# Zeroing the rows behind an expert buffer's overflow in another stage, as copies from DRAM to DRAM

## The chip, the core and the metric

The kernel runs on one core of a Trainium2 chip. The metric is device time in microseconds (us) of one execution. The core has five instruction queues that run side by side and meet only through semaphores: PE (matrix multiply, with its weight loads shown as PEld), DVE (vector), ACT (activation), POOL (general, and here the indirect DMAs) and SP, which only issues DMAs. The DMAs of all queues are carried by the same 16 DMA engines.

## The reference, cut to what matters

```python
x = attention(q, k_pooled, v_pooled)             # 4608 tokens x 512
logits = x @ w_gate + log1p(exp(x @ w_noise)) * noise
top2 = two best of 8 experts per token, softmax over the two -> gates
for e in range(8):                               # mixture of experts
    out[mask_e] += gate * (relu(x[mask_e] @ w1[e]) @ w2[e])   # 512 -> 1024 -> 512
h = out @ w_in                                   # 512 -> 2048, float64 weights
return (h * cos(h)) @ w_out                      # 2048 -> 512
```

## The kernel before

There are three stages.

**Attention, about 0 to 340 us.** Four groups of nine token tiles. The code works in 20 units `u` of one or two tiles; the order of the work inside a unit is a fixed list, and small steps for the next group are filled in between. SP loads k, v and q of later groups; POOL scatters each finished token row to its two experts' places in the DRAM buffer `xs` (indirect DMAs, line 588). Between units, SP also writes zeros. `zero_x` (line 218) clears the ends of the eight expert areas in `xs`. `zero_y(i)` (line 222) is called twice after each of the units 4 to 12, 18 times in all. Each call writes 384 rows of 2 KB, 768 KB, into the part of `yb` that begins at row `YS`; the source is the zero tile `zt` in on-chip memory (SBUF), 128 partitions each giving three rows. The 18 calls cover all 54 x 128 overflow rows.

**Experts, about 340 to 1075 us.** Each expert has 1216 places (`CAP`), worked as jobs of 512, 512 and 192 rows. Tokens beyond an expert's places are overflow: a loop (line 811) runs once for every 128 of them, `nov` times in all (a count that is read at run time), and writes its result to `yb` from row `YS` on. In a job, `mm1` (line 611, eight blocks `f`) makes `ph`, ACT turns it into the high half of `ht` (line 887) and DVE into the low half (line 888); `mm2` (line 900) makes `py`, which ACT scales (903) and stores into `yb` (905). The jobs' inputs come by `DMA_TRANSPOSE xt<-xs` (867), the experts' weights by lines 129 to 133.

The list `work` holds the calls of `mm1` and `mm2` in order, two blocks of the next job's `mm1` between two tiles of `mm2`. `begin` is the PE time at which each of them should start by a count of columns, and `at(t, f)` puts step `f` behind the first piece of work that begins at or after `t`. That way the background steps are spread: the splitting of the next expert's weights, and `bg`, the preparation of the last stage's float64 weights. A chunk of these is loaded by SP into `yg` (956), POOL makes `tm` from it (966), DVE converts it (973 to 976), ACT and DVE split it into `ty` (1022, 1023), and SP stores that into `wind` or `woutd` (1024). All queues run in order, so a background step that waits holds up whatever stands behind it on its engine.

**Last stage, about 1075 us to the end.** Per four tiles POOL gathers the two expert rows of each token from `yb` (1097; the first two groups from the rows of the 512-row jobs, the later ones from all of `yb`), then the two dense layers follow on PE (1315 and 1352).

SP's and ACT's DMAs take eight completion semaphores in turn. A DMA is issued only when the one that had its semaphore before it has landed.

Of the kernel before, what the change touches and what calls it, by code (L numbers as in the profile page):

```python
# [8 lines left out]
F32 = mybir.dt.float32  # L9
# [11 lines left out]
NTOK, DM, E, F, DFF = 4608, 512, 8, 1024, 2048  # L21
# [3 lines left out]
YS = E * CAP  # L25
ZROW = 960
OVT = 54
# [8 lines left out]
def tile_attn_moe_ffn(ctx: ExitStack, tc: tile.TileContext, q, k, v, wgate, wnoise, noise,  # L36
                      w1, w2, win, wout, out):
    nc = tc.nc
    V, A, PL, PE, SP = nc.vector, nc.scalar, nc.gpsimd, nc.tensor, nc.sync

    def dap(src, offset, dims):
        return bass.AP(tensor=src.tensor, offset=src.offset + offset, ap=dims)

    const = ctx.enter_context(tc.tile_pool(name="const", bufs=1))
    dram = ctx.enter_context(tc.tile_pool(name="dram", bufs=1, space=DR))
    ctx.enter_context(tc.manual_schedule())

    xs = dram.tile([E * ER, 2 * DM], F16, name="xs")
    yb = dram.tile([YS + 128 * OVT, DM], F32, name="yb")
    idx = const.tile([128, G, 2, R], I32, name="idx")  # L50
    yidx = const.tile([128, G, 2, R], I32, name="yidx")
    gates = const.tile([128, G, 2, R], F32, name="gates")
# [20 lines left out]
    def load_kv(g, which):  # L73
        src, dst = ((k, KT), (v, VT))[which]
        t = ow.tile([128, 5, 2, 512], F32, name="w1", bufs=2)
        for c in range(5):
            n = 128 if c < 4 else 64
            for h in range(2 if which and c == 4 else 1):
                SP.dma_start(t[64 * h:64 * h + n, c, :, :],
                             dap(src, 2 * g * S * 512 + 65536 * c, [[512, n], [S * 512, 2], [1, 512]]))  # L80
        dst[g] = t
# [84 lines left out]
    def w2_room(e):  # L166
        return SW[:, 0:4096].bitcast(F16) if e % 2 == 0 else WP[1]
# [46 lines left out]
    zt = ac.tile([128, 2048], F16, name="zt")  # L214
    V.memset(zt, 0.0)

    def zero_x():
        SP.dma_start(dap(xs, ZROW * 1024, [[2048, 128], [ER * 1024, 8], [1, 2048]]),
                     zt[:, None, :].to_broadcast([128, 8, 2048]))

    def zero_y(i):
        SP.dma_start(dap(yb, (YS + 384 * i) * 512, [[512, 128], [65536, 3], [1, 512]]),
                     zt.bitcast(F32)[:, None, 0:512].to_broadcast([128, 3, 512]))

    def pow2(pool, m, bits, nm):

# [356 lines left out]
    def scatter(g, r):  # L583
        def f():
            xr = XR.pop(g * R + r)
            for kk in range(2):
                PL.memset(spacer, 0.0)
                st = PL.indirect_dma_start(
                    out=xs[:, :], out_offset=bass.IndirectOffsetOnAxis(ap=idx[:, g, kk, r:r + 1], axis=0),
                    in_=xr.rearrange("p s a h d -> p (s a h d)"), in_offset=None)  # L590
                for o in SCAT:
                    tc.declare_no_dep(st.ins, o.ins, reason="each slot is written once")
                if "load" in EARLY:
                    tc.declare_no_dep(st.ins, EARLY["load"].ins, reason="rows of later pairs lie behind the first chunk")
                SCAT.append(st)
        return f
# [33 lines left out]
    def with_ups(gt, fs):  # L630

        return gt[:6] + [early_up(f) for f in fs] + gt[6:9] + [early_lo(f) for f in fs] + gt[9:]
# [30 lines left out]
    def mix(a, b):  # L663

        n = len(a) + len(b)
        out, i, j = [], 0, 0
        while i < len(a) or j < len(b):
            if j >= len(b) or (i < len(a) and i * len(b) <= j * len(a)):
                out.append(a[i])
                i += 1  # L670
            else:
                out.append(b[j])
                j += 1
        return out
# [14 lines left out]
    def go():  # L689
        k_ = -(-len(fill) // left[0])  # L690
        left[0] = max(left[0] - 1, 1)
        for f in fill[:k_]:
            f()
        del fill[:k_]

    for u in range(NU):
        g, r, n = UNITS[u]
        it = u % 5
        if it == 0:
            a = []  # L700
            if g + 1 < G:
                pk, kt_, pv, sv = setup_steps(g + 1)
                a = pk + pv[:2]
                for i in range(4):
                    a += kt_[i:i + 1] + pv[i + 2:i + 3]
                a += sv
                if g + 2 < G:
                    a.append(lambda g=g: (load_kv(g + 2, 0), load_kv(g + 2, 1)))
            if g == G - 1:
                a = p2  # L710
            fill += mix(a, late)
            late = []
        if g == G - 2 and it == 2:
            p1, p2 = prep_steps(0, "w1"), prep_steps(0, "w2")
            p1.pop(0)()
            p2.pop(0)()
        if g == G - 2 and it == 3:
            fill = mix(fill, p1)
        if g == G - 1 and it in CUTS:
            r0, r1 = CUTS[it]  # L720
            gt = gating(g, r0, r1)
            gt.pop(0)()
            fill += with_ups(gt, (0, 1) if it == 3 else (2, 3)) + [scatter(g, r_) for r_ in range(r0, r1)]
        left[0] = ORDER.count("G") * ((5 if g < G - 1 or it > 2 else 3) - it)
        if g == G - 1 and it == 3:
            left[0] = 6
        for op in ORDER:
            k_ = int(op[1:] or 0)
            if op == "A0":

                while first_v:
                    first_v.pop(0)()
            if op[0] == "G":
                go()
            elif op[0] == "S":
                scores(u + 2, k_)
            elif op[0] == "E":
                expo(u + 2, k_)
            elif op[0] == "N":
                soft_sum(u + 1)  # L740
            elif op[0] == "T":
                e_tr(u, k_)
            elif op[0] == "A":
                av(u, k_ // 2, k_ % 2)
            else:
                q_tr(u + 3, k_)
        if u == 2:
            zero_x()
        if 4 <= u <= 12:
            zero_y(2 * u - 8)  # L750
            zero_y(2 * u - 7)
        if it == 4:
            assert not fill
            if g + 2 < G:
                load_q(g + 2)
            if g == G - 2:
                early_load()
            if g < G - 1:
                late = gating(g, 0, R)
                late.pop(0)()  # L760
                late += [scatter(g, r_) for r_ in range(R)]
# [48 lines left out]
    nov = nc.values_load(novi[0:1, 0:1], min_val=0, max_val=OVT)  # L810
    with tc.For_i(0, nov, 1) as i:
# [4 lines left out]
        p = PT[0]()  # L816
# [10 lines left out]
        z = wp.tile([128, 1024], F16, name="x2h", bufs=2)  # L827
# [265 lines left out]
    def gather(c, i):  # L1093
        g, r = CHF[c][i]
        yg = wp.tile([128, 2, 512], F32, name="yg", bufs=4)
        for kk in range(2):
            PL.indirect_dma_start(out=yg[:, kk, :], out_offset=None, in_=yb[0:512 * E * (c + 1), :] if c < 2 else yb[:, :],
                                  in_offset=bass.IndirectOffsetOnAxis(ap=yidx[:, g, kk, r:r + 1], axis=0))
        CB["yg", c, i] = yg

# [120 lines left out]
    for j in range(1, NJ + 1):  # L1221
        up_ = [(mm1, j, f) for f in range(8)] if j < NJ else []
        dn = []
        if j > 0:
            e, c = JOBS[j - 1]
# [10 lines left out]
    first = {e: min(i for i, w_ in enumerate(work) if w_[0] is mm1 and JOBS[w_[1]][0] == e) for e in range(E)}  # L1236
    first[E] = len(work)
    sched = [[] for _ in work]
    begin = [0.0]
# [3 lines left out]
    def at(t, f):  # L1243

        sched[min(i for i in range(len(work)) if begin[i] >= t)].append(f)
# [11 lines left out]
    for f in bg:  # L1257
        for r0, r1 in rest:
            if r0 <= b0 < r1:
                b0 += r1 - r0  # L1260
        at(b0, f)
        b0 += each
    FW = {}

    def load_out(i):
        def f():
            t = w2_room(i).rearrange("p (k n) -> p k n", n=512)
            FW.setdefault("out", []).append(t)
            SP.dma_start(t.rearrange("p k f -> p (k f)"), woutd[:, i, :])
        return f  # L1270

    def load_in(i):
        def f():
            o, n = ((0, 10), (10, 9), (19, 9))[i]
            t = ow.tile([128, n, 1024], F16, name="st" if i else "w1", bufs=2)
            FW.setdefault("in", []).extend(t[:, j, :] for j in range(n))
            SP.dma_start(t, wind.rearrange("p o s k f -> p (o s k) f")[:, o:o + n, :])
# [10 lines left out]
    o = work.index((mm2, JOBS.index((E - 1, 0)), 3))  # L1288
# [18 lines left out]
    def prod(c, q_, n, ps, start):  # L1307
        a_, b_ = PRODS[n]
        x = xt_tile(c, b_).rearrange("p (i s k) n -> p i s k n", i=2, s=2)
        for h in range(2):  # L1310
            f = 128 * (2 * q_ + h)
            o = ps[:, 256 * h:256 * h + 256].rearrange("p (i n) -> p i n", i=2)
            for k_ in range(2):
                for j, (sa, sb) in enumerate(((0, 0), (0, 1), (1, 0))):
                    PE.matmul(o, FW["in"][4 * a_ + 2 * sa + k_][:, f:f + 128], x[:, :, sb, k_, :],  # L1315
                              start=(start and h == 0 and k_ == 0 and j == 0), stop=(k_ == 1 and j == 2), skip_group_check=True)
# [27 lines left out]
    def down(c, q_, b, tt, h):  # L1344

        def f():
# [4 lines left out]
            for i, (a_, b_) in enumerate(((0, 0), (0, 1), (1, 0))):  # L1351
                PE.matmul(ps, g[:, 2 * b + a_, 256 * h + 128 * tt:256 * h + 128 * tt + 128], FW["out"][b_][:, k_, :],  # L1352
                          start=(q_ == 0 and b < 2 and h == 0 and i == 0), stop=(q_ == 3 and b > 1 and h == 1 and i == 2))
# [105 lines left out]
```

## Time and profile before

| | us |
|---|---|
| median of 3 runs | 1832.84 |
| lowest and highest | 1831.86, 1833.45 |
| the profiled execution | 1835.67 |
| its span (first to last instruction) | 1833.9 |
| PE busy in the span | 1737.3 (95%) |
| DVE, ACT, POOL busy | 1063.2, 927.0, 424.3 |

The profiled execution lies 2.8 us above the median. PE's chain of work makes up most of the span: of the chain that ended last, 76% is PE. DMA engines are busiest in the first tenth of the span and then between 20 and 100% over the experts stage. DMA-issuing instructions are not counted as busy time of an engine; the trace shows when each was issued, and how long the issuing queue was held by it.

### The profile page before, as it was taken

Reading aid. Unit: us, or ns where it says so; the run is one execution under the profiler, and the core shown is the slowest. Engines: PE = TensorE matmul, PEld = TensorE weight load, DVE = VectorE, ACT = ScalarE, POOL = GpSimd, SP = SyncE. Lnnn points to the kernel's source line nnn. Section 1 sums busy time; section 2 is a strip of 40 time slices with the busy share of each in tenths; the row PEclk is TensorE's granted clock in tenths of the full one; section 3 lists DMA queues with packets and bytes.
Section 4 is the critical chain, followed back from the end, with each engine's and each line's share of the span. In section 5 each row is a group of like instructions: output and inputs, shape, how many; then the busy total and the mean of one; then the engine's idle time right before and its main releaser. Section 6 shows DMA issues by size and latency. Waiting matters only on the chain.

```text
span 1833.9 us, 28207 instructions
## 1 busy us (share of the span) xinstructions
PE 1737.3 (95%) x11113; PEld 1024.7 (56%) x11113; DVE 1063.2 (58%) x2018; ACT 927.0 (51%) x1843; POOL 424.3 (23%) x458
## 2 busy tenths in 40 slices
PE   5977777899999999999999998999999999999999
PEld 3655554355444644464445545666666666666665
DVE  7685765363567376525775134756656556565633
ACT  4765553232324233323333235777776777777765
POOL 1225437100001000000110012424333342433222
PEclk9888778899999999999999999999999999999999
DMA  9977424548353837466463635304232141322200
GB/s 277 307 261 273 174 92 161 153 159 229 107 180 117 243 107 219 125 178 167 132 212 90 215 127 144 79 32 87 63 71 59 52 87 41 75 64 64 41 24 24
DMA packets 233208, 243.49 MB, mean 133 GB/s; under 512 B 154352, under 2 KB 167664, under 8 KB 232432
## 3 DMA queue, kind: packets, MB, share of 16 engines
q1 hardware_dynamic: 210544, 183.97, 35.7%
q0 software_dynamic: 11520, 37.76, 6.3%
q10 hardware_dynamic: 11008, 19.93, 3.1%
q8 instruction: 88, 1.44, 0.3%
q14 instruction: 48, 0.39, 0.1%
HBM read 127.06 MB, written 78.12 MB: 112 GB/s over the span
## 4 chain that ended last, share of the span: by engine, by line
PE 76%; DVE 3%; ACT 1%; issue 1%; ACTq 0%; DVEq 0%
PE ph L1352 20%; PE py L900 19%; PE ph L611 18%; PE py L1315 15%; PE pt L1315 3%; PE py L915 1%; DVE w L159 1%; DVE ht L888 0%; DVE x L1112 0%; ACT w L158 0%; DVE amw L139 0%; DVE ty L1327 0%; DVE ty L974 0%; DVE ty L976 0%; DVE ty L975 0%
## 5 line engine op out<-in xcount | busy, mean ns | idle before, releaser
L611 PE MATMUL ph<-xt,w 128*128 128x512 f16 (+1 forms) x2208 | 387.1, 333 | 1.0 <-DVE ht L888 1.0
L1352 PE MATMUL ph<-sw,ht 128*128 128x512 f16 x1152 | 383.0, 379 | 0.0
L611 PEld LDWEIGHTS <-w 128*128 128x128 f16 x2304 | 214.4, 98 | 187.3 <-issue 6.1
L1342 POOL TENSOR_TENSOR ht<-ty,ht 128x512 f16<-128x512 f32 x144 | 183.6, 1281 | 479.9 <-ACT ht L1341 324.0
L900 PEld LDWEIGHTS <-ht 128*128 128x128 f16 x1632 | 159.4, 98 | 187.6 <-DVE ht L888 0.7
L888 DVE SCALAR_TENSOR_TENSOR ht<-ph,ht 128x512 f16<-128x512 f32 (+2 forms) x184 | 104.0, 568 | 259.5 <-ACT ht L887 259.4
L1352 PEld LDWEIGHTS <-ht 128*128 128x128 f16 x1728 | 169.3, 98 | 152.1 <-issue 0.8
L1352 PE MATMUL ph<-w,ht 128*128 128x512 f16 x576 | 218.6, 379 | 0.0
L1315 PEld LDWEIGHTS <-st 128*128 128x128 f16 x1872 | 183.2, 98 | 54.4 <-issue 3.5
L900 PE MATMUL py<-w,ht 128*128 128x512 f16 x864 | 191.9, 379 | 0.0
L887 ACT ACTIVATE ht<-ph 128x512 f16<-128x512 f32 (+2 forms) x184 | 91.5, 498 | 164.2 <-PE ph L611 148.5
L900 PE MATMUL py<-sw,ht 128*128 128x512 f16 x768 | 171.2, 379 | 0.2 <-DVE ht L888 0.2
L903 ACT ACTIVATE yt<-py,ysc 128x512 f32<-128x512 f32 x72 | 49.3, 685 | 229.6 <-PE py L900 229.5
L1315 PE MATMUL py<-xt,st 128*128 128x256 f16 x1040 | 139.3, 273 | 3.1 <-ACT ht L1405 3.1
L1327 DVE SCALAR_TENSOR_TENSOR ty<-ty,k,ht 128x512 f32<-128x512 f32 x108 | 93.7, 868 | 81.7 <-ACT ty L1321 80.0
L1336 DVE SCALAR_TENSOR_TENSOR ty<-ty,ht 128x512 f32<-128x512 f32 x108 | 74.7, 692 | 108.7 <-ACT ty L1333 105.6
L1315 PEld LDWEIGHTS <-w 128*128 128x128 f16 x1152 | 113.1, 98 | 39.6 <-issue 3.8
L1332 ACT ACTIVATE ty<-ty,k 128x512 f32<-128x512 f32 x144 | 102.8, 714 | 21.4 <-DVE ty L1327 21.3
L1315 PE MATMUL py<-w,st 128*128 128x256 f16 x832 | 111.8, 273 | 0.0
L1321 ACT ACTIVATE ty<-ht,k 128x512 f32<-128x512 f32 x108 | 77.4, 717 | 67.3 <-DVE ht L1406 33.8
L1341 ACT ACTIVATE ht<-ty 128x512 f16<-128x512 f32 x144 | 89.5, 622 | 34.9 <-DVE ty L1336 34.3
L966 POOL TENSOR_TENSOR tm<-yg 128x512 f32<-128x512 f32 x32 | 33.7, 1053 | 297.0 <-DVE x L976 183.5
(262 smaller groups left out, 2366.8 us busy)
## 6 DMA issues: line engine op xcount, KB each, us to landing
yb<-yt ACTq DMA_DIRECT2D x72, 256.0 KB
yg<-in_moe_w_in_dram SPq DMA_DIRECT2D x32, 512.0 KB
yg<-in_moe_w_out_dram SPq DMA_DIRECT2D x32, 512.0 KB
st<-in_moe_w_dram SPq DMA_DIRECT2D x7, 2048.0 KB
yb<-zt SPq DMA_DIRECT2D x18, 768.0 KB
st<-in_moe_w_dram SPq DMA_DIRECT2D x8, 1536.0 KB
w<-in_k_dram SPq DMA_DIRECT2D x16, 512.0 KB
w<-in_v_dram SPq DMA_DIRECT2D x16, 512.0 KB
```

Source lines behind the costliest of these rows:

```text
L611: PE.matmul(ps[:, 0:n], w[:, a_, k_, 128 * f:128 * f + 128], xt[:, 4 * b_ + k_, 0:n], start=(i == 0), stop=(i == 11))
L887: A.activation(t[:, 0], p, AF.Relu)
L888: V.scalar_tensor_tensor(t[:, 1], p, 0.0, t[:, 0], op0=OP.max, op1=OP.subtract)
L900: PE.matmul(ps[0:m], ht[:, a_, f, 128 * t:128 * t + m], w[:, b_, f, :], start=(i == 0), stop=(i == 23))
L1315: PE.matmul(o, FW["in"][4 * a_ + 2 * sa + k_][:, f:f + 128], x[:, :, sb, k_, :], start=(start and h == 0 and k_ == 0 and j == 0), stop=(k_ ...
L1321: A.activation(y, h, AF.Identity, bias=CB["k4", c][:, 0:1])
L1327: V.scalar_tensor_tensor(y, y, CB["k4", c][:, 0:1], h, op0=OP.subtract, op1=OP.subtract)
L1332: A.activation(y, y, AF.Sin, scale=CB["k4", c][:, 1:2])
L1336: V.scalar_tensor_tensor(UB[b][3], UB[b][3], CC, UB[b][2], op0=OP.subtract, op1=OP.mult)
L1341: A.activation(g[:, 2 * b, :], y, AF.Copy)
L1342: PL.tensor_sub(g[:, 2 * b + 1, :], y, g[:, 2 * b, :])
L1352: PE.matmul(ps, g[:, 2 * b + a_, 256 * h + 128 * tt:256 * h + 128 * tt + 128], FW["out"][b_][:, k_, :], start=(q_ == 0 and b < 2 and h == ...
```

## The change

`zero_y` now writes to a place that is known only at run time: the 384 rows that begin `nov * 128` rows behind `YS + 384 * i`. So the rows that the overflow loop wrote are left alone and as many rows behind the old end of the buffer are written; `yb` is made 54 x 128 rows longer for that. The source is a new 256 KB DRAM buffer `zd` of zeros, filled once from `zt` after unit 2, and each of the 18 copies reads it three times. The copies are placed with `at` in the experts stage, evenly between the begin of expert 1 and the begin of expert 7. The gathers of the last stage read the old extent of `yb`.

```diff
-    yb = dram.tile([YS + 128 * OVT, DM], F32, name="yb")
+    yb = dram.tile([YS + 256 * OVT, DM], F32, name="yb")
+    zd = dram.tile([128, DM], F32, name="zd")
...
+    def zero_d():
+        SP.dma_start(zd[:, :], zt.bitcast(F32)[:, 0:512])
+
+    ZY = []
+
     def zero_y(i):
-        SP.dma_start(dap(yb, (YS + 384 * i) * 512, [[512, 128], [65536, 3], [1, 512]]),
-                     zt.bitcast(F32)[:, None, 0:512].to_broadcast([128, 3, 512]))
+        def f():
+            z = SP.dma_start(yb[bass.ds(nov * 128 + (YS + 384 * i), 384), :].rearrange("(k p) d -> k p d", p=128),
+                             zd[None, :, :].to_broadcast([3, 128, DM]))
+            for o in ZY:
+                tc.declare_no_dep(z.ins, o.ins, reason="rows behind those of the overflow")
+            ZY.append(z)
+        return f
...
         if u == 2:
             zero_x()
-        if 4 <= u <= 12:
-            zero_y(2 * u - 8)
-            zero_y(2 * u - 7)
+            zero_d()
...
-in_=yb[0:512 * E * (c + 1), :] if c < 2 else yb[:, :],
+in_=yb[0:512 * E * (c + 1), :] if c < 2 else yb[0:YS + 128 * OVT, :],
...
         b0 += each
+    z0, z1 = begin[first[1]], begin[first[E - 1]]
+    for i in range(18):
+        at(z0 + (z1 - z0) * i / 18, zero_y(i))
     FW = {}
```

No instruction of PE, DVE, ACT or POOL changes its place; SP's queue is the one that differs. In the attention stage of the kernel before, the zero writes stand between the loads of q (`st<-in_q_dram`), k and v:

```order
L79 DMA w_1007<-in_v_dram 64x2x512 x2
L222 DMA yb<-zt 128x3x512 x2
L88 DMA st<-in_q_dram 64x8x576 x2
L222 DMA yb<-zt 128x3x512 x8
L79 DMA w_1971<-in_k_dram 128x2x512 x4
L79 DMA w_1971<-in_k_dram 64x2x512
```

In the changed kernel the same place of SP's queue holds the loads alone (the numbers in the names are buffer numbers):

```order
L80 DMA w_1009<-in_v_dram 64x2x512 x2
L89 DMA st<-in_q_dram 64x8x576 x2
L80 DMA w_1963<-in_k_dram 128x2x512 x4
L80 DMA w_1963<-in_k_dram 64x2x512
```

The ten writes of this place are gone from it, and the loads follow one another.

In the experts stage, where expert 7's weights are loaded and the chunks of `w_out` are prepared, SP's queue before is:

```order
L131 DMA st<-in_moe_w_dram 128x3x1024
L133 DMA st<-in_moe_w_dram 64x1024 x2
L1024 DMA woutd<-ty 256x1x512
L956 DMA yg<-in_moe_w_out_dram 128x1024
L129 DMA st<-in_moe_w_dram 128x8x512
L1024 DMA woutd<-ty 256x1x512
L956 DMA yg<-in_moe_w_out_dram 128x1024
```

The same place in the changed kernel:

```order
L132 DMA st<-in_moe_w_dram 128x3x1024
L134 DMA st<-in_moe_w_dram 64x1024 x2
L1033 DMA woutd<-ty 256x1x512
L965 DMA yg<-in_moe_w_out_dram 128x1024
L130 DMA st<-in_moe_w_dram 128x8x512
L1033 DMA woutd<-ty 256x1x512
L229 ISA
L229 DMA yb<-zd 3x4x16384
L965 DMA yg<-in_moe_w_out_dram 128x1024
```

A register instruction and a copy (the sixteenth of the 18) now stand directly ahead of a `yg` load. The copy's shape is three outer rows of four pieces of 16384 numbers of four bytes, where the write before had 128 outer rows. The next copy stands in the same way ahead of a `yg` load, and the last one ahead of an `xt` load:

```order
L965 DMA yg<-in_moe_w_out_dram 128x1024
L1033 DMA woutd<-ty 256x1x512
L229 ISA
L229 DMA yb<-zd 3x4x16384
L965 DMA yg<-in_moe_w_out_dram 128x1024
L1033 DMA woutd<-ty 256x1x512
L965 DMA yg<-in_moe_w_out_dram 128x1024
L1033 DMA woutd<-ty 256x1x512 x3
L229 ISA
L229 DMA yb<-zd 3x4x16384
L876 DMA_TRANSPOSE xt<-xs 128x8x512
```

## Rows read from the trace of the kernel before

**Rows 1.** Busy time by stage: PE, PEld, DVE, ACT, POOL, PEclk, DMA share, GB/s.

```profile
0.00:350.00 350.00, 265.25 (x2235) 175.52 (x2236) 232.52 (x684) 184.68 (x653) 133.85 (x208) 0.83 0.66 210
350.00:1075.00 725.00, 723.86 (x3928) 364.37 (x3926) 395.25 (x661) 225.99 (x360) 39.97 (x41) 1.00 0.56 166
1075.00:1834.00 759.00, 748.15 (x4954) 484.81 (x4951) 435.44 (x673) 516.38 (x831) 250.52 (x210) 1.00 0.26 65
```

**Rows 2.** PE's waits, 340 to 1075 us: us in total, times, longest.

```profile
PE py L900 <- DVEq L811: 3.8, 1, 3.8
PE ph L611 <- DVE ht L888: 1.0, 1, 1.0
PE py L900 <- DVE ht L888: 0.2, 1, 0.2
```

**Rows 3.** The one wait for a DMA in the attention stage, in PE's timeline.

```profile
30.48 1.06 PE L365 MATMUL tr<-idf,st 128*128 128x128 f32 x8 [2.60 <-DMA st<-in_q_dram]
```

**Rows 4.** SP's queue, the zero writes: first and last; then their issue times.

```profile
76.74 1.68 SPq L222 DMA_DIRECT2D yb<-zt  x2
...
206.30 3.63 SPq L222 DMA_DIRECT2D yb<-zt  x2
...
L222 SPq DMA_DIRECT2D yb<-zt x18: 389/1873/10150, 76.7 to 207.9; - x18
```

**Rows 5.** Two stretches of steady large DMAs, columns as in Rows 1.

```profile
100.00:112.00 12.00, 7.41 (x86) 5.38 (x85) 11.41 (x31) 6.58 (x26) 2.12 (x1) 0.92 1.02 392
1014.00:1030.00 16.00, 16.00 (x76) 7.25 (x74) 2.77 (x5) 3.08 (x5) 0.00 (x0) 1.00 0.98 410
```

**Rows 6.** Four of 18 equal stretches between expert 1 and expert 7, same columns.

```profile
419.00:452.00 33.00, 32.24 (x202) 16.88 (x202) 11.49 (x20) 6.60 (x13) 0.00 (x0) 1.00 0.97 261
...
452.00:485.00 33.00, 33.00 (x155) 15.06 (x154) 20.53 (x33) 11.00 (x15) 0.00 (x0) 1.00 0.44 128
...
917.00:950.00 33.00, 33.00 (x155) 15.04 (x153) 22.31 (x35) 10.46 (x16) 4.16 (x4) 1.00 0.65 230
950.00:983.00 33.00, 33.00 (x162) 15.63 (x161) 27.82 (x42) 11.38 (x17) 3.12 (x3) 1.00 0.39 109
```

**Rows 7.** SP's queue where the last three copies will stand.

```profile
918.71 2.60 SPq L1024 DMA_DIRECT2D woutd<-ty  x1
921.41 1.18 SPq L956 DMA_DIRECT2D yg<-in_moe_w_out_dram  x1
...
959.15 0.55 SPq L956 DMA_DIRECT2D yg<-in_moe_w_out_dram  x1
...
992.98 4.94 SPq L867 DMA_TRANSPOSE xt<-xs  x1
```

**Rows 8.** POOL's timeline there, and its waits from 850 to 1000 us.

```profile
932.83 1.04 POOL L966 TENSOR_TENSOR tm<-yg 128x512 f32<-128x512 f32 x1 [7.05 <-DMA yg<-in_moe_w_out_dram]
...
965.72 1.04 POOL L966 TENSOR_TENSOR tm<-yg 128x512 f32<-128x512 f32 x1 [7.79 <-DVE ty L976]
...
POOL tm L966 <- DMA yg<-in_moe_w_out_dram: 18.4, 3, 7.1
```

**Rows 9.** DVE's timeline around these two chunks.

```profile
934.37 0.42 DVE L973 TENSOR_SCALAR ty<-yg 128x512 int32<-128x512 int32 x1
...
936.36 0.69 DVE L976 SCALAR_TENSOR_TENSOR ty<-tm,ty 128x512 f32<-128x512 f32 x1
...
939.96 0.69 DVE L888 SCALAR_TENSOR_TENSOR ht<-ph,ht 128x512 f16<-128x512 f32 x1 [1.24 <-ACT ht L887]
```

**Rows 10.** PE's timeline where these jobs' `mm2` begin, and expert 7's `mm1`.

```profile
941.83 5.34 PE L900 MATMUL py<-sw,ht 128*128 128x512 f16 x24
...
978.20 3.74 PE L611 MATMUL ph<-xt,w 128*128 128x512 f16 x24
981.78 5.13 PE L900 MATMUL py<-sw,ht 128*128 128x512 f16 x23
987.08 0.39 PE L900 MATMUL py<-sw,ht 128*128 128x512 f16 x1 [0.17 <-DVE ht L888]
...
1017.54 19.28 PE L611 MATMUL ph<-xt,w 128*128 128x512 f16 x96
```

**Rows 11.** Busy time between these points, columns as in Rows 1.

```profile
941.00:959.00 18.00, 18.00 (x85) 8.20 (x84) 13.67 (x21) 8.42 (x11) 2.08 (x2) 1.00 0.40 110
959.00:987.00 28.00, 27.91 (x138) 13.09 (x135) 22.40 (x36) 10.32 (x14) 2.08 (x2) 1.00 0.34 104
```

More of the change, by code (lines that the diff above doesn't have):

```diff
@@ L1096, in gather @@
         for kk in range(2):
-            PL.indirect_dma_start(out=yg[:, kk, :], out_offset=None, in_=yb[0:512 * E * (c + 1), :] if c < 2 else yb[:, :],
+            PL.indirect_dma_start(out=yg[:, kk, :], out_offset=None, in_=yb[0:512 * E * (c + 1), :] if c < 2 else yb[0:YS + 128 * OVT, :],
                                   in_offset=bass.IndirectOffsetOnAxis(ap=yidx[:, g, kk, r:r + 1], axis=0))
```

## The prediction

> **What bounds the kernel now.** I read the busy times by stage first. In the experts stage PE is busy for 723.86 of 725 us at a granted clock of 1.00, in the attention stage for 265.25 of 350 us at 0.83 [rows 1]. So a microsecond that PE loses in the experts stage is lost to the whole kernel, and one that the attention stage gains counts only if something there waited for what is removed. Second, I read who made PE wait in the experts stage: DVE, for 1.2 us in all besides the 3.8 us at the overflow loop [rows 2]. Third, the waits of the attention stage that a DMA ended: there is one, of 2.60 us at 30.48 us, for a load of q [rows 3]. Last, the DMA share: the 18 zero writes go out between 76.74 and about 210 us [rows 4], while the engines are full for stretches (1.02 at 392 GB/s) [rows 5], and in the stretches of the experts stage to which they move the share runs from 0.39 to 0.97 [rows 6].
>
> **What is removed.** 18 writes of 768 KB leave the attention stage. While they queue, the median one holds SP for 1.873 us [rows 4], which is 768 KB at about 420 GB/s, so all 16 engines carry each. That frees 18 x 1.87 = 34 us of DMA time. What it buys is a matter of waits: the only DMA wait that PE has in that stage ends 46 us before the first zero write, and DVE's, ACT's and POOL's waits of that stage name no DMA. I take 0 for this term. The loads of k, v and q then land earlier than needed. It could be more than 0 only through a wait that the trace does not name; a loss I exclude, since nothing is added there but one 256 KB write, a third of one of the removed ones.
>
> **What is added on queues.** SP gets 18 register instructions and 18 copies; SP is no compute engine, and its own issuing time is at nothing as long as the loads behind land in time. That is the question.
>
> **One copy's time on the DMA engines.** The trace has no copy from DRAM to DRAM and no DMA with fewer than 64 outer rows, so I bound it. The order rows show three outer rows of four 64 KB pieces. Lower end: the data spread as the writes before, 1.9 us. Upper end: one engine for each outer row, 256 KB each. In a stretch of large loads 16 engines at share 0.98 move 410 GB/s, 26.1 GB/s for one; in the zero writes 392 / 16 / 1.02 = 24.0 [rows 5]. 256 KB at 24 to 26 GB/s is 10.0 to 10.9 us, on three engines. I take the upper end, 10 us, because the outer count, 3 in place of 128, is what differs between the two instructions, and three rows cannot go evenly to more than three engines. Every other DMA uses all 16 and is complete only when its slowest engine is, so anything queued behind a copy lands up to 10 us later.
>
> The Trainium skill has a rule for this ("DMA: Bandwidth & Descriptors", section "Why a DMA increments its semaphore by 16 and not by 1"): a DMA runs on the largest number of engines up to 16 that divides the outermost dimension of both sides. By that rule the copies run on three engines and the writes before on 16, so the sum below would stand and the first rival would fall; no row of this trace has a DMA on fewer engines.
>
> **Load on those three engines.** 18 x 10 = 180 us over the 598 us between 419 and 1017 us adds 0.30 to a mean share of 0.555 over the 18 stretches, whose lowest and highest are of the kind shown [rows 6]. Only the stretches with an expert's weights (0.97 the highest) go over 1, and each is followed by one near 0.44 that takes the backlog. So delays stay near 10 us and don't pile up.
>
> **What stands behind the copies.** Most loads have room: the `xt` load at 992.98 is used at 1017.54 [rows 7, 10], and its 4.94 us of issue plus 10 us of delay leave more than 9 us. The chunks of `w_out` do not. POOL waits for three of them to land, 18.4 us in all [rows 8], so there each microsecond of delay goes on to POOL, from POOL to DVE's lines 973 to 976, and DVE's line 888, which makes `ht` for PE, stands behind these.
>
> - Sixteenth copy, ahead of the load at 921.41 [rows 7]. POOL started on that chunk at 932.83, as soon as it landed [rows 8]; 10 us later is 942.8. DVE, which reached it at 934.37, does line 976 some 7 us late after 936.36 moves to about 943.5, and the `ht` of 939.96 comes near 947 [rows 9]. PE's `mm2` group of 941.83 runs 5.34 us and needs this last block of `ht` in its last eighth, from 946.5 on [rows 10]. PE loses about 2 us.
> - Seventeenth copy, ahead of the load at 959.15 [rows 7]. POOL used that chunk at 965.72 [rows 8]; the load takes some 4 to 5 us, so there is 2 us of room, and 8 are left. DVE is busy for 22.40 of the 28 us from there to 987 [rows 11], and part of the first delay is still in it (13.67 of 18 us busy before that). It regains about 2 us by 987. There PE waits for DVE already, by 0.17 us [rows 10]. PE loses about 6 us.
> - The other sixteen. Where DVE is late by less than the room that a job's change gives (3.74 us of `mm1` and most of 5.13 us of `mm2` [rows 10]) nothing is lost; four more stand close ahead of a chunk that POOL or DVE takes soon. I allow 0.5 us each, 2 us together, at most 3 us each.
>
> ACT could also be held: a store's issue waits for the DMA eight places before. Eight places are some 16 us of queue in this stage, more than a copy's 10; I take 0, at most 3 us at each of the three bursts of weights, 9 together.
>
> **The sum.** 0 - 0 + 2 + 6 + 2 = 10 us on the profiled execution's 1835.67 us, 1845.7. That execution lies 2.8 us above the median of the runs, so on the median's scale: 1832.84 + 10 = 1843 us. With the small ends, 4 us; with the large ones 8 + 12 + 9, about 29: from 1837 to 1862 us.
>
> **Rivals.**
> - *The copies spread over all engines after all.* Then one costs 1.9 to 2.5 us (twelve pieces of 64 KB, one on each of twelve engines at 26 GB/s, are 2.5 us). The load at 921.41 makes POOL 2 us late, the room at the job's change swallows that, and about 0 to 2 us is left at 987: 1833 to 1835 us, the same within what can be measured. For it speaks that every DMA in the trace is spread; against it the three outer rows. This is decided at about 5 us per copy.
> - *Three engines at half the rate*, because each has to read and write the same memory. 20 us a copy is 360 us in 598, 0.60 on top of 0.555: the three engines are over full by 0.16 x 598 = 94 us in the worst case, and loads fall behind for hundreds of microseconds. With 10 us more at six copies it is 60 us: 1893 us. For it: no row shows an engine reading and writing DRAM at once. Against it: the writes before ran at 24 GB/s per engine, near the rate of loads.
> - *The attention stage gains.* PE is idle for 85 us there [rows 1], and the writes took 34 us of full engines. If loads or scatters that the trace doesn't name gate it, 5 us or more could come back while the copies stay hidden: 1828 us. Against it: no wait names a DMA after 30.48 us.
>
> The Trainium skill speaks for the second rival ("DMA: Bandwidth & Descriptors", section "Latency and other measured facts"): it gives 214 GB/s per direction as the full rate of copies within DRAM, from which an estimate of 13.4 GB/s per engine and 20 us per copy follows. No run here shows it; the sum would be about 60 us by it.
>
> **How the numbers follow.** Forecast 0.43; copies spread 0.29; half rate 0.12; attention gains 0.10; three engines, but all of it absorbed, 0.06 (no change). What a measurement can tell from no change is 0.2%, 3.7 us. Slower: 0.43 + 0.12 = 0.55; same: 0.29 + 0.06 = 0.35; faster: 0.10. The range takes in the spread copies and the large ends, and the lower part of the half-rate case: 1830 to 1880 us; the forecast's own is 1837 to 1862.
>
> **What would show it.** In the profile after: `yg` loads behind a copy landing some 10 us later than before, POOL's `tm` waiting for them for longer than 18.4 us, and new waits of PE for DVE's line 888 near 946 and 987 us, with PE still near 1.00 of the clock; the attention stage ending at the same 340 us, with a DMA share near 0.5 between 78 and 210 us. The forecast is wrong if PE's waits in the experts stage stay near 1 us (spread, or absorbed), if `xt` loads come late or the share of the three engines runs full for long (half rate), or if the first `mm2` moves ahead of 342 us by more than 3 us.

## The result, and the profile after

The changed kernel takes 1853.82 us (median of 4 runs, 1850.77 to 1856.35), the kernel before 1832.35 us (4 runs beside them): a ratio of 1.0115, 95% interval 1.0098 to 1.0132. It is slower by 21 us. The sign and the mechanism of the forecast (a copy sits on three DMA engines for some 10 us) hold; the size was 10 us, and the places where the time goes are mostly others than those named. The profiled execution took 1852.71 us, with a span of 1850.9 us.

Busy time of the first two stages of the changed kernel, columns as in [rows 1] (the last stage takes 761 us where it took 759):

```profile
0.00:350.00 350.00, 269.95 (x2272) 176.37 (x2273) 232.28 (x684) 186.13 (x655) 134.12 (x208) 0.84 0.61 178
350.00:1090.00 740.00, 722.61 (x3885) 361.77 (x3884) 395.63 (x661) 224.73 (x358) 40.02 (x40) 0.99 0.67 178
```

In the experts stage PE is idle for 17.4 of 740 us, where it was for 1.1 of 725 [rows 1], and the granted clock is 0.99 instead of 1.00. Who made PE wait there (us in total, times, longest), beside [rows 2]:

```profile
PE pt L113 <- DVE mbc L107: 12.9, 3, 5.0
PE py L909 <- DVEq L820: 3.8, 1, 3.8
PE ph L622 <- DMA xt<-xs: 3.5, 1, 3.5
PE ph L622 <- DVE ht L897: 1.0, 1, 1.0
```

The overflow loop's 3.8 us and the 1.0 us for `ht` are as before. New are three waits for `mbc` and one for `xt`. Taking each ACT instruction's start, after minus before, at the same place of the program, I get the loss place by place: 6.2 us at the first wait (571 us in the changed kernel), 7.3 at the second (745), 4.6 at the third (980), 5.9 at the last (1024), 0.5 elsewhere, 24.6 in all. The spans differ by less, 17.0 us, because in these two profiles the changed kernel was 7.9 us earlier out of the attention stage. It got ahead between 144 and 172 us, where the kernel before ran twice at the lower clock and the changed kernel did not (it did so in other places: over the whole stage the granted clock is 0.83 and 0.84). One of these stretches, before and after in turn; 158 to 165 us reads the same, 0.52 and 1.00:

```profile
144.00:151.00 7.00, 7.00 (x51) 5.10 (x49) 2.11 (x8) 3.53 (x15) 6.21 (x13) 0.52 1.06 357
```

```profile
144.00:151.00 7.00, 6.49 (x70) 4.84 (x71) 3.26 (x11) 5.57 (x21) 5.99 (x13) 1.00 1.05 318
```

**The first wait, step by step.** SP's queue ahead of the copy of 527.26 us (the fourth, number 3 from 0), its waits there, and the stores of `yt` on ACT's queue:

```profile
500.30 0.52 SPq L132 DMA_DIRECT2D st<-in_moe_w_dram  x1
500.87 8.96 SPq L134 DMA_DIRECT2D st<-in_moe_w_dram  x2
515.29 0.34 SPq L965 DMA_DIRECT2D yg<-in_moe_w_in_dram  x1
526.66 0.38 SPq L130 DMA_DIRECT2D st<-in_moe_w_dram  x1
527.26 0.80 SPq L229 DMA_DIRECT2D yb<-zd  x1
528.19 0.35 SPq L965 DMA_DIRECT2D yg<-in_moe_w_in_dram  x1
528.63 5.25 SPq L1033 DMA_DIRECT2D wind<-ty  x4
```

```profile
SPq L130 <- DMA yb<-yt: 11.0, 1, 11.0
SPq L134 <- DMA yb<-yt: 7.9, 1, 7.9
SPq L965 <- DMA yb<-yt: 5.4, 1, 5.4
```

```profile
502.80 0.34 ACTq L914 DMA_DIRECT2D yb<-yt  x1
513.16 0.34 ACTq L914 DMA_DIRECT2D yb<-yt  x1
523.52 0.34 ACTq L914 DMA_DIRECT2D yb<-yt  x1
```

SP stood still for 24.3 us, each time for a store of y that ACT had not yet issued when SP came to its load: SP's next DMA counts on the same one of the eight completion semaphores. The stores of 513.16 and 523.52 landed 2.06 and 3.08 us after their issue and SP went on within 0.1 us, so in these two waits, 16.4 us together, it is not the DMA engines that held SP but the place in the order. (The store of 502.80 took 6.5 us to land, behind SP's own loads.) In the whole experts stage SP waited for such stores for 68.8 us in all, against 2.3 us before. The largest of its five rows, and the only one before:

```profile
SPq L965 <- DMA yb<-yt: 23.9, 7, 9.2
```

```profile
SPq L129 <- DMA yb<-yt: 2.3, 1, 2.3
```

In the end a 2 MB load of weights, the copy, a `yg` load and three `wind` stores go out within 4 us, at 526.66 to 530.3. The `wind` stores landed at 547.06 to 548.43, some 18 us after their issue. Where they were late can be read from the semaphores: such a store raises its semaphore 16 times in the trace, a copy of 3 rows only four times, once 1.2 us after its issue and three times when it lands (544.5 to 544.7 us here). Of the first `wind` store thirteen increments came by 537.4 us and the last three at 546.9 to 547.1. (Where the copy at this place has 6 rows, in "thirteen long" below, ten come by 532.9 and six at 537.2 to 538.1.) ACT, DVE and PE follow:

```profile
547.14 0.72 ACT L1031 ACTIVATE ty<-x,turns 128x512 f16<-128x512 f32 x1 [8.13 <-DMA wind<-ty]
```

```profile
547.90 0.75 DVE L1032 SCALAR_TENSOR_TENSOR ty<-x,turns,ty 128x512 f16<-128x512 f32 x1 [6.96 <-ACT ty L1031]
...
570.94 0.23 DVE L107 COPY mbc<-amw 128x128 f32<-128x128 f32 x1
```

```profile
571.22 0.33 PE L113 MATMUL pt<-idf,mbc 128*128 128x128 f32 x1 [4.32 <-DVE mbc L107]
571.38 4.44 PE L622 MATMUL ph<-xt,w 128*128 128x512 f16 x12
575.66 5.34 PE L909 MATMUL py<-sw,ht 128*128 128x512 f16 x24
```

ACT needs the buffer of `ty` that the late store still reads, DVE idles 6.96 us behind ACT, does not regain it all in 23 us, and is late with `mbc`, the input of a small transpose that stands in PE's own queue (`bcast2`, the scale of the next expert's weights). PE waits 4.32 us and then runs 12 matmuls in 4.44 us, when 24 of the same size right behind take 5.34. The granted clock there (the first line), right behind it at full speed again (the second), and around or behind the other three waits:

```profile
571.00:575.00 4.00, 3.78 (x10) 1.47 (x11) 2.74 (x9) 1.15 (x1) 1.04 (x1) 0.57 0.20 79
575.00:590.00 15.00, 15.00 (x81) 7.56 (x80) 11.05 (x16) 6.75 (x10) 1.78 (x2) 1.00 0.05 19
742.00:749.00 7.00, 4.08 (x11) 1.55 (x12) 5.67 (x13) 1.15 (x1) 0.00 (x0) 0.51 0.90 255
981.00:985.00 4.00, 4.00 (x12) 1.46 (x11) 3.02 (x7) 1.21 (x2) 0.00 (x0) 0.57 0.32 127
1025.00:1029.00 4.00, 4.00 (x13) 1.45 (x12) 0.00 (x0) 0.47 (x1) 0.00 (x0) 0.57 0.88 327
```

So each wait is paid again in part: of the 24.6 us, 16.4 are the four new waits (12.9 + 3.5) and most of the other 8.2 is PE at the lower of its two levels (an estimate: the four stretches at that level last 17.1 us, of which PE was busy for about 14).

**The second, third and last.** At the second, SP, DVE and PE show the same picture with a load of `w_out` (copy 9 at 722.82, behind a load of weights that SP's waits had brought to 719.83):

```profile
742.00 0.69 DVE L1000 TENSOR_REDUCE fm<-yg 128x1 f32<-128x512 f32 x1 [9.98 <-DMA yg<-in_moe_w_out_dram]
```

```profile
744.92 0.47 PE L113 MATMUL pt<-idf,mbc 128*128 128x128 f32 x1 [5.03 <-DVE mbc L107]
...
979.74 0.33 PE L113 MATMUL pt<-idf,mbc 128*128 128x128 f32 x1 [3.54 <-DVE mbc L107]
...
1024.28 4.21 PE L622 MATMUL ph<-xt,w 128*128 128x512 f16 x12 [3.52 <-DMA xt<-xs]
```

The third is the place of the forecast's sixteenth copy: POOL waits for the chunk behind it for 18.18 us, where the longest wait was 7.1 [rows 8]:

```profile
952.89 1.22 POOL L975 TENSOR_TENSOR tm<-yg 128x512 f32<-128x512 f32 x1 [18.18 <-DMA yg<-in_moe_w_out_dram]
```

The last is `xt` of expert 7, whose issue stands right behind copy 17:

```profile
1003.20 0.78 SPq L229 DMA_DIRECT2D yb<-zd  x1
1004.09 18.53 SPq L876 DMA_TRANSPOSE xt<-xs  x2
```

### The profile page after: what moved, and what is told of

Its sections match the earlier page's. It is cut to its first block, busy times and chain, and to the rows that moved or that the text cites. A ratio compares the mean times of both kernels' runs of the same rounds, so it can differ in the third digit from the quotient of the medians.

```text
span 1850.9 us, 28251 instructions
## 1 busy us (share of the span) xinstructions
PE 1740.5 (94%) x11113; PEld 1022.8 (55%) x11113; DVE 1064.1 (57%) x2018; ACT 928.3 (50%) x1843; POOL 426.0 (23%) x458
## 4 chain that ended last, share of the span: by engine, by line
PE 71%; DMA 4%; DVE 4%; ACT 1%; issue 1%; SPq 0%; ACTq 0%; DVEq 0%
PE ph L1364 20%; PE py L909 17%; PE ph L622 16%; PE py L1327 15%; PE pt L1327 2%; DMA yg<-in_moe_w_out_dram 2%; PE py L924 1%; DMA xt<-xs 1%; DMA wind<-ty 1%; DVE amw L140 1%; DVE w L160 0%; DVE ht L897 0%; DVE x L1121 0%; DVE ty L1339 0%; ACT ty L1031 0%
## 5 line engine op out<-in xcount | busy, mean ns | idle before, releaser
L622 PE MATMUL ph<-xt,w 128*128 128x512 f16 (+1 forms) x2208 | 393.9, 336 | 4.5 <-DMA xt<-xs 3.5
```

The lines of the kernel that those rows point to most:

```text
L622: PE.matmul(ps[:, 0:n], w[:, a_, k_, 128 * f:128 * f + 128], xt[:, 4 * b_ + k_, 0:n], start=(i == 0), stop=(i == 11))
```

## The experiments

Each kernel is compared with the kernel before on the same chip; the chips differ (the kernel before takes 1807.6, 1808.2, 1834.3 and 1807.7 us in the four groups below), so only ratios and differences within a group count, and the times in us that the first group's expectations name are those of the chip of the result. "Place" means the four places above, measured in each profile in the same way.

**First group: what removing, traffic and the number of outer rows do.** Theory: the loss is the time of a copy on three engines. Rival: it is the traffic added to the experts stage.

No copies at all (the calls of `zero_y` are taken out, and the gathers of the last stage read `yb` up to row `YS` only; so also in the kernels with five, thirteen and tiny copies below):

```diff
-    for i in range(18):
-        at(z0 + (z1 - z0) * i / 18, zero_y(i))
```

> Leaves out the zeroing of the overflow rows altogether (no write in the attention stage, no copy in the experts stage; the gathers read yb up to row YS only). Both theories of the copies (few engines, or traffic) expect the experts stage as before the change: 725 us, PE's waits in it near 1 us. On the attention stage two theories differ. If the removed writes held it up, expert work begins near 335 us as in the changed kernel (343 us before) and the time is 1824 to 1826 us. If those 8 us were the luck of the granted clock, it begins within 3 us of 343 in the median and the time is 1830 to 1834 us.

1808.99 us against 1807.62, 1.0005 (0.9995 to 1.0015). This is the second of the two theories on the attention stage: taking the writes out of the attention stage is worth nothing.

The same copies, bytes and places with 16 outer rows of 48 KB, with 6 of 128 KB, and with 12 of 64 KB:

```diff
-  ...rearrange("(k p) d -> k p d", p=128), zd[None, :, :].to_broadcast([3, 128, DM]))
+  ...rearrange("(k p) d -> k p d", p=24), zd[None, 0:24, :].to_broadcast([16, 24, DM]))   # 16 rows
+  ...rearrange("(k p) d -> k p d", p=64), zd[None, 0:64, :].to_broadcast([6, 64, DM]))    # 6 rows
+  ...rearrange("(k p) d -> k p d", p=32), zd[None, 0:32, :].to_broadcast([12, 32, DM]))   # 12 rows
```

> The changed kernel with the same 18 copies at the same places, but each as 16 outer rows of 48 KB in place of 3 outer rows of 256 KB. Few engines: a copy takes about 1.9 us on all 16 engines, PE's waits in the experts stage fall from 20 us to under 3 us, and the time comes within 2 us of the kernel without any zeroing. Traffic (14.2 MB read and written beside the experts' loads, and 18 more places in SP's queue): as the changed kernel, 1848 to 1855 us.

> The changed kernel with each copy as 6 outer rows of two 64 KB pieces. Few engines: two pieces of 2.43 us one behind the other, 4.9 us a copy; loads that had 2 to 4 us of room are late by half as much as with three rows: 3 to 10 us above the kernel without zeroing. Traffic: as the changed kernel, 1848 to 1855 us.

> The changed kernel with each copy as 12 outer rows of one 64 KB piece. Few engines: 2.4 us a copy on twelve engines, 0 to 3 us above the kernel without zeroing. Traffic: as the changed kernel, 1848 to 1855 us.

Measured: 16 rows 1.0005 (0.9994 to 1.0016), 12 rows 1.0001 (0.9990 to 1.0012), 6 rows 1.0011 (1.0001 to 1.0021), 2 us. Six rows cost less than expected (0.8 us above the kernel without copies, where 3 to 10 were); the traffic rival falls, since all of them move the same bytes. Experts stage without copies and with 16 rows:

```profile
350.00:1050.00 700.00, 698.55 (x3810) 352.73 (x3809) 383.35 (x634) 221.34 (x352) 41.65 (x42) 1.00 0.56 167
```

```profile
350.00:1050.00 700.00, 698.70 (x3811) 352.68 (x3810) 383.69 (x634) 221.48 (x352) 42.19 (x42) 1.00 0.62 187
```

The DMA share goes from 0.56 to 0.62 and PE loses nothing.

**Second group: which copies.** The changed kernel again; five copies alone; the other thirteen alone; and 2 outer rows of 384 KB, so that each of two engines has six pieces.

```diff
-    for i in range(18):
+    for i in (3, 9, 15, 16, 17):                               # five
+    for i in (0, 1, 2, 4, 5, 6, 7, 8, 10, 11, 12, 13, 14):     # thirteen
...
-  ...rearrange("(k p) d -> k p d", p=128), zd[None, :, :].to_broadcast([3, 128, DM]))
+  ...rearrange("(k p) d -> k p d", p=192), zd[None, 0:192, :].to_broadcast([2, 192, DM]))   # two rows
```

For the two rows `zd` is 192 rows long and is filled by two writes, so that kernel has one DMA more.

> The changed kernel as it stands (3 outer rows of 256 KB per copy, all eighteen), beside the kernels that follow, on the same chip. Two profiles of another chip put its loss in the experts stage at 24 us, of which 7.9 us were hidden by a clock fall of the kernel before in attention that the kernel without copies does not gain back. Both theories: 15 to 25 us above the kernel before, ratio 1.008 to 1.014.

> Only the copies 3, 9, 15, 16 and 17 of the changed kernel (numbered from 0), the other thirteen left out; the unzeroed rows are not gathered. Theory 'few loads without room': each copy costs TensorE only where a load stands right behind it whose user comes within some 25 us, and these five are the places where the changed kernel's trace lost time (6.2, 7.2, 4.6 and 5.9 us, 24 in all with the clock that falls after each stall): 12 to 24 us above the kernel before, at least 70% of what the whole change costs. Rival 'load of the three engines': every copy takes a share of the engines that all loads cross, and what is late is the sum: five of eighteen, 28%, some 6 us.

> The other thirteen copies alone (0 to 2, 4 to 8, 10 to 14). Theory 'few loads without room': 0 to 5 us above the kernel before, no TensorE wait above 2 us in the experts stage. Rival 'load of the three engines': 72% of the cost of the whole change, some 15 us.

> All eighteen copies with 2 outer rows of 384 KB each, so two engines with six pieces of 64 KB one behind the other: 6 x 2.43 = 14.6 us a copy instead of 9.7, same bytes and places. Both theories: more than the changed kernel. The room theory: each place lost 4 to 5 us of room past its slack at 9.7 us, so 5 us more at each of four or five places and a few new ones: 20 to 45 us above the changed kernel, with more TensorE waits on DVE's mbc. If the time of a copy did not matter: same as the changed kernel.

Measured: the changed kernel 1831.73 against 1808.18, 1.0140 (1.0123 to 1.0157), 23.5 us; five 1.0038 (1.0024 to 1.0053), 7.5 us; thirteen 1.0008 (0.9998 to 1.0018), 0.9 us; two rows 1.0323 (1.0307 to 1.0339), 58.5 us. Two rows lie 35 us above the changed kernel, within the 20 to 45 expected. But five and thirteen are both cheap, and 7.5 + 0.9 is far from 23.5, so neither theory holds as it stood. The five alone lose nothing at the first place. There SP's queue, its waits on DMAs and PE read:

```profile
484.92 0.39 SPq L130 DMA_DIRECT2D st<-in_moe_w_dram  x1
485.54 0.93 SPq L229 DMA_DIRECT2D yb<-zd  x1
492.78 0.36 SPq L965 DMA_DIRECT2D yg<-in_moe_w_in_dram  x1
507.94 4.89 SPq L1033 DMA_DIRECT2D wind<-ty  x3
```

```profile
SPq L965 <- DMA yb<-yt: 6.2, 1, 6.2
```

```profile
549.24 0.27 PE L113 MATMUL pt<-idf,mbc 128*128 128x128 f32 x1
```

Here the loads of weights are not held: the copy goes out 22 us ahead of the `wind` stores instead of 1.4 us, and they pass freely. That gave a new theory: the loss needs both a copy of 3 rows at the place and SP's loads held back until they stand beside it.

**Third group: the same order, other durations.** The kernels with 6 outer rows count each of the 425 DMAs of SP and ACT on the same semaphore as the changed kernel does, so a mixture changes the time of the copies and nothing of the order.

```diff
+            k = 3 if i in (3, 9, 15, 16, 17) else 6        # five long
+            k = 3 if i not in (3, 9, 15, 16, 17) else 6    # thirteen long
+            k = 3 if i < 17 else 6                         # last short
...
```

`k` is the number of outer rows; the same 384 rows are written at the same places.

> All eighteen copies, so the same DMAs with the same semaphores as in the changed kernel; copies 3, 9, 15, 16 and 17 with 3 outer rows, the other thirteen with 6 (half the time on an engine). New theory 'held back, then behind a long copy': SP's and ACT's DMAs share eight semaphores, and with eighteen more DMAs in that order SP's loads wait for y stores that ACT issues later (in the changed kernel the st, yg and wind loads around 500 us stood until a copy of 3 rows was just ahead of them; with five copies alone they did not). It needs both, the order of eighteen and a long copy at the place: 16 to 24 us above the kernel before, with TensorE waits on mbc of 4 to 5 us near 547 and 722 us. Rival 'load of the three engines piles up from copy to copy': the thirteen short ones leave half the load, so about what five alone cost (7.5 us) and at most 12.

> The reverse: copies 3, 9, 15, 16 and 17 with 6 outer rows, the other thirteen with 3. 'Held back, then behind a long copy': the places that hurt have a short copy: 1 to 6 us above the kernel before. Rival 'load piles up': thirteen of eighteen long ones, 12 to 20 us.

> The changed kernel with only the last copy (17) in 6 outer rows. It stands ahead of the load of xt for the last expert, for which the changed kernel's TensorE waited 3.5 us in one profile and 1.2 us in another, and then ran 1.7 to 3.4 us at the lower clock. If the last copy costs that: 2 to 6 us below the changed kernel (ratio 1.010 to 1.013 against the kernel before). If xt is late from what stands earlier: no change from the changed kernel, 1.014.

Measured against 1834.26 us: five long 1855.60, 1.0125 (1.0095 to 1.0156); thirteen long 1831.32, 0.9988 (0.9968 to 1.0008); only the last short 1848.91, 1.0089 (1.0062 to 1.0115). Five long lie 21 us above the kernel before, as expected. Thirteen long miss the 1 to 6 us expected on the low side. The last short lies 6.7 us below five long; the changed kernel itself was not run in this group. (The 1.7 us at the lower clock that the expectation for it counts are not in the trace: behind the wait of 1.2 us the granted clock was 1.00.) The first place with five long (SP's wait, PE), and then with thirteen long:

```profile
SPq L130 <- DMA yb<-yt: 10.9, 1, 10.9
```

```profile
578.29 0.36 PE L113 MATMUL pt<-idf,mbc 128*128 128x128 f32 x1 [4.20 <-DVE mbc L107]
...
751.64 0.48 PE L113 MATMUL pt<-idf,mbc 128*128 128x128 f32 x1 [4.83 <-DVE mbc L107]
```

```profile
SPq L130 <- DMA yb<-yt: 11.0, 1, 11.0
```

```profile
562.24 0.33 PE L113 MATMUL pt<-idf,mbc 128*128 128x128 f32 x1
...
730.18 0.33 PE L113 MATMUL pt<-idf,mbc 128*128 128x128 f32 x1 [0.41 <-DVE mbc L107]
```

SP is held for 11 us in both; PE waits only where the copy at the place is long. Thirteen long copies of eighteen cost nothing that can be measured, so load that piles up is out.

**Fourth: five long copies among thirteen that move next to nothing.**

```diff
+            k, n = (3, 384) if i in (3, 9, 15, 16, 17) else (6, 6)
...
```

> All eighteen DMAs again, copies 3, 9, 15, 16 and 17 with 3 outer rows as in the changed kernel, but the other thirteen move six rows of 2 KB each instead of 384 rows (the rest of their rows stays unzeroed and is not gathered), so they put nothing that counts on the DMA engines and only stand in the order. 'Held back, then behind a long copy': the order alone holds the loads, so 16 to 26 us above the kernel before (the kernel whose thirteen others had half the time: 21), steps of 5 to 8 us near 550 and 722 us. If the traffic of the thirteen others is part of the cause: 7 to 12 us, as the five alone (7.5), with little or no step near 550 and 722 us. In between, 12 to 16 us, would say both.

1815.82 against 1807.69 us, 1.0048 (1.0035 to 1.0060): 8 us, as with the five alone, and not the 16 to 26 expected. Taken by its number it would speak for the traffic of the thirteen. The trace says that it doesn't tell: with other sizes the build dealt the semaphores differently (292 of 425 as in the changed kernel), and SP's loads at the first place were not held:

```profile
479.81 0.39 SPq L130 DMA_DIRECT2D st<-in_moe_w_dram  x1
480.42 2.97 SPq L230 DMA_DIRECT2D yb<-zd  x1
488.59 0.35 SPq L966 DMA_DIRECT2D yg<-in_moe_w_in_dram  x1
502.92 9.21 SPq L1034 DMA_DIRECT2D wind<-ty  x4
```

So my sentence "the order alone holds the loads" was too simple: it is which semaphore each DMA counts on, and eighteen copies do not fix that. A hold without the thirteen's traffic was not reached. But the packets of the changed kernel's trace show that none of the thirteen is on an engine there: copy 2's last piece ends at 481.4 us, copy 3's first begins at 534.0, and copy 4's first at 559.2, when the `wind` stores have landed. With copy 4 long and copy 3 short ("thirteen long") 0.2 us is lost at the first place. So there the thirteen count through the order that they give, not through the bytes that they move.

Kernels by place (us lost, each profile against that of before; "held" is SP's 11 us wait ahead of the place of copy 3). With 12 and 16 rows at most 1.1 us is lost at any place, with two rows 58.8 us in all:

| kernel | held | copy 3 | 1st | 2nd | 3rd | last |
|---|---|---|---|---|---|---|
| changed, first chip | yes | 3 rows | 6.2 | 7.3 | 4.6 | 5.9 |
| changed, second group | yes | 3 rows | 6.5 | 9.5 | 4.8 | 2.9 |
| last short | yes | 3 rows | 7.4 | 7.7 | 4.8 | 1.4 |
| five long, rest 6 rows | yes | 3 rows | 6.1 | 7.2 | 4.4 | 6.3 |
| thirteen long, rest 6 rows | yes | 6 rows | 0.2 | 1.3 | 0.7 | 0.3 |
| all 6 rows | yes | 6 rows | 0.1 | 0.4 | 0.7 | 0.3 |
| thirteen alone | yes | none | 0.0 | 1.1 | 0.0 | 0.2 |
| five alone | no | 3 rows | 0.0 | 1.0 | 1.3 | 6.4 |
| five long, rest tiny | no | 3 rows | 0.0 | 0.7 | 0.7 | 5.6 |
| none | no | none | 0.0 | 0.0 | 0.0 | 0.3 |

The loss of the first column is there only with both. The second and third columns go the same way, 4.4 to 9.5 us with both and at most 1.3 us otherwise, though the waits of SP there are others than the one in the table. The last place needs no hold: it is copy 17 alone.

## Why the prediction was right, and where it was not

- *Removed writes, 0.* Right: 1.0005 (0.9995 to 1.0015) with neither the old writes nor the copies. The first profile ended its attention stage 7.9 us earlier, which by the forecast's last paragraph would have spoken against it; that was how this one pair of executions went (its rows show the clock), not the writes. In the three profiles of the third group, whose attention stage has no zero writes either, it ended 0.7, 1.6 and 12.5 us earlier than in the profile of before (on another chip, where the kernel before takes 1834.3 us).
- *A copy takes 10 us on three engines.* Right. The packet records show 216 packets of 65,536 bytes, twelve for each copy, with a median of 2.425 us; four behind one another are 9.7 us. A copy's semaphore is raised once right after the issue and then 3 times; with 2, 6 and 12 rows 2, 6 and 12 times, and with 16 rows 16 times in all. Fewer pieces for each engine (6, 12 or 16 rows) cost 0 to 2 us, more (2 rows, six pieces, 14.6 us) 58.5 us. The rule of the Trainium skill ("DMA: Bandwidth & Descriptors", section "Why a DMA increments its semaphore by 16 and not by 1") that the outer count sets the number of engines agrees with these counts and this order. The rival at half rate falls: a piece moves at 65,536 / 2.425 us = 27.0 GB/s on its engine, both reading and writing DRAM. In the kernel with 16 rows a piece of 48 KB takes 1.83 us, 26.9 GB/s on each of sixteen engines. The estimate of 13.4 GB/s, from the same page's figure for copies within DRAM (section "Latency and other measured facts"), fits neither of the two; the measurement decides.
- *The load of the three engines doesn't pile up.* Right: thirteen long copies of eighteen, 0.9988 (0.9968 to 1.0008).
- *Sixteenth and seventeenth copies, 2 + 6 us through `ht`.* At the sixteenth's place 4.6 us were lost (1.3 and 0.7 in the kernels without the hold), the seventeenth cost no wait of PE, and the route was wrong. The `yg` load behind the seventeenth landed at 985.1 us, after PE's wait at 979.74, and PE waited for nothing from there to the last place. The load behind the sixteenth landed at 952.75. PE's waits for `ht` stayed at 1.0 us; what came late was `mbc`, 27 us further on in DVE's queue (979.46), for which PE's queue holds a transpose. I had followed DVE's instructions to the one that feeds the matmuls and passed over the ones that feed the preparation of the next weights.
- *The other sixteen, 2 us together.* This is the step that failed: 13.5 us at the first two places. The failure is in the sentence on the semaphores: I asked whether a store of ACT's would wait for a DMA eight places before, and took 0. (I reckoned eight places as 16 us; in the trace before they are 24 us at the median and 8.8 at the least.) It went the other way round: SP's loads waited for ACT's stores, 68.8 us in all against 2.3 us before, though each copy is one DMA among 425. The rows that I read [rows 7] show when SP issued, and I carried these times over to the changed kernel as if 18 more DMAs only added their own.
- *The last copy leaves more than 9 us.* Wrong: 5.9 us, and 1.4 with that copy in 6 rows. The room was counted to 1017.54 [rows 10], where a long run of `mm1` begins; PE's first use of that `xt` lies 7.8 us ahead, at 1009.8 in the kernel before: the group that begins at 1008.78 ends with twelve matmuls on it, which take 2.75 of its 3.74 us.

```profile
1008.78 3.74 PE L611 MATMUL ph<-xt,w 128*128 128x192 f16 x24
```

  And the issue of the load took 15.8 us behind the copy, not 4.94, so it landed later than the 10 us of the forecast. A late `xt` was the forecast's sign for the half rate; the 2.425 us of a piece rule that out.
- *PE stays near 1.00 of the clock.* It does between the waits; with each wait of 3.5 to 5 us it fell to the lower level for several microseconds, and the forecast had no such term. It is most of 8.2 of the 24.6 us.

So the forecast's range held the result for a reason that covers half of it: the copy's length. That the range reached so far was luck: its upper end came from allowances for other waits (9 us for ACT's stores, 12 us for four chunks) than those that came. The sum was mis-sized because the places were judged one by one from the times at which SP had issued before.

What stays open: why the build deals the semaphores in one way for 3 and 6 outer rows and in another for 12, 16 or tiny copies; the order with 3 rows but without the hold at both first places was not tried except with five copies and with thirteen tiny ones beside them.

## What to carry to other kernels

A DMA's outer count is part of its cost: here a copy of 768 KB in 3 outer rows held three engines for 9.7 us and eighteen of them cost 21 to 24 us, in 12 or 16 rows nothing that could be measured, and none of these versions beats the kernel before, because nothing waited for the writes that were moved. When a DMA is added to a queue that shares a few completion semaphores with another engine's, look in SP's waits for stores that SP did not wait for before: its issue times, and with them the room of every load behind, may shift; here three such waits in a row made 24 us, and two of them were the order alone. Follow a late engine to everything that it feeds on the critical engine, small transposes of the next stage's preparation included.

## What the runs showed of the hardware

- With each of the four waits of 3.5 to 5.0 us in the changed kernel's profile PE's granted clock fell from 2.4 to 1.2 GHz for 3.4 to 6.8 us before it rose again (0.57 and 0.51 in the stretches above); the wait of 1.0 us for `ht` had no such effect, and neither had one of 3.39 us in the kernel with five long copies (at 986.46, granted clock 1.00 behind it). In this profile the waits cost about half of themselves again.
- A 64 KB piece copied within DRAM ran at 27.0 GB/s on one DMA engine, no slower than loads do (26.1 GB/s [rows 5]), and 48 KB pieces on sixteen engines at 26.9 GB/s each.
- A store issued 1.4 us behind such a copy landed in two parts: thirteen of its sixteen increments by 537.4 us, three at 546.9 to 547.1, right behind the copy's three (544.5 to 544.7).
- The time of a copy at the place decides steeply: 4.85 us for each copy (two pieces, by the same 2.425 us) cost 2 us in all, 9.7 us cost 23.5, 14.6 us cost 58.5.
